# Sliding-window attention with a channel mix: crossbar transposes for two more batches, other loads for batch 0, mix copies shared between two engines, new orders

## The chip, the cores and the metric

One core of one Trainium2 chip. The metric is the device time of one launch in microseconds (us), lower is better. The engines are TensorE (PE, its weight load is PEld), VectorE (DVE), ScalarE (ACT), GpSimd (POOL) and SyncE (SP); SP issues hardware DMAs, POOL issues software DMAs, which can change the type on the way.

## The reference

Eight batches, eight heads, 576 positions, head size 64. Attention first, then a channel mix on its output (all inputs are fp32):

```python
scores = scale * q @ k.T ; bias = -slope[h] * |i - j| ; mask = 0 <= i - j < 128
attn = softmax(where(mask, scores + bias, -1e9)) ;  a = attn @ v
x = a.transpose(0, 2, 1, 3).reshape(B, S, 512)
x_prev = x shifted by one position, zero first
xk = mu_k * x + (1 - mu_k) * x_prev ;  xr = mu_r * x + (1 - mu_r) * x_prev
out = sigmoid(xr @ w_r) * (relu(xk @ w_k) ** 2 @ w_v)
```

## The kernel before, in words

**Pairs.** Attention works on pairs of heads: pair `it` is batch `it // 4`, group `it % 4`, 32 pairs in all. For each pair: scores in two halves (`scores` L229 with the distance bias as a matmul on L217 for batch 0; `scores4` L242, L247 for batches 2 and later), `expo` (L263) on ScalarE, `masked` (L271) on VectorE from batch 1 on, `av` (L287), then `norm`: a reciprocal of the row sums (L297) and a multiplication (L298) into the tile xu.

**From xu to the mix.** The normalised pair must be turned, so that features lie on partitions. In batches 0 to 3 (`NXB = 4`) TensorE does it with five 128x128 transposes (`x_transp`, L306) into PSUM, and ScalarE copies the result to xt (`x_copy`, L317). From batch 4 on one DMA through the crossbar does both (`x_cross`, L311, issued by SP). Then, on VectorE, `delta` (L330) is x less x shifted by one, `scaled` (L336) makes the two copies mu_k * delta and mu_r * delta, and `mix` (L347) adds the shifted x and writes xm, the input of the channel mix. In batch 0 the pair goes through this in two halves, of 256 and 320 positions.

**Units.** Two batches (1152 positions) make one P, 0 to 3. `mm1` (L359) multiplies by w_k in pieces of columns (four of 256, 256, 256, 384 in P = 0, then 512, 384, 256), eight output blocks each; `relu` (L365) on ScalarE; `square` (L372 on ScalarE or L374 on VectorE); `mm3` (L381) and `gate` (L387); `mm2` (L396); `product` (L402) on VectorE; `store` (L408) on SP.

**q and k.** From batch 2 on POOL loads them with a cast, VectorE turns them (`turn` L180, `turn_tail` L188) and SP shifts the turned queries with a DMA within SBUF (`shift`, L196, qt<-qt in the profile). In batches 0 and 1 TensorE transposes them (`qk_transp`) and ScalarE or VectorE copies them out of PSUM (L132, L129). Pair 0 alone (`NHW = 1`) comes as fp32 by SP (L93) and is cast on VectorE (L129); pairs 1 to 3 come cast, by POOL (L108, L124).

**Buffers.** Four PSUM banks "mm" serve transposes, mm1, mm2 and mm3 in turn; two pairs of banks "sa" serve scores and av. Delta and scaled copies have a ring of three tiles each, relu's tile rl four, the output tile ot three, xu three.

**Order.** The order on each engine is written out by hand in the tables ORDER (one list of names for each of PE, ACT, DVE, POOL, SP); a planner merges the lists with the dependences and gives out ring slots. `tq.5` is the transpose of pair 5's queries, `rl.0.256.3` the relu of P 0, columns from 256, block 3; `fill` is two matmuls on a tile of zeros. Whether a square runs on ScalarE is told by the list that holds its name. An engine works through its list strictly: an instruction that waits holds all behind it.

Of the kernel before, what the change touches and what calls it, by code (L numbers as in the profile page):

```python
# [16 lines left out]
def kernel(  # L17
# [12 lines left out]
    nc = tc.nc  # L30
# [16 lines left out]
    NXB = 4  # L47
# [6 lines left out]
    NHW = 1  # L54
# [5 lines left out]
    rlp = ctx.enter_context(tc.tile_pool(name="rlp", bufs=4))  # L60
    otp = ctx.enter_context(tc.tile_pool(name="otp", bufs=3))
# [21 lines left out]
    ldr = xk_buf[1][:, 0:2048].bitcast(FP32).rearrange("p (i g h c) -> p i g h c", i=2, g=NHW, h=2)  # L83
    ts_buf = xk_buf[1][:, 2048:2560].rearrange("p (h d) -> p h d", h=H)
    tt_buf = xk_buf[1][:, 2560:3328].rearrange("p (g t c) -> p g t c", g=G, t=3)
    cs_buf = [xr_buf[1][:, 1024 * i:1024 * i + 1024].rearrange(
        "p (i r h d) -> p i r h d", i=2, r=NF, h=2) for i in range(NHW)]
    dl_buf = [cst.tile([128, S], BF16, name=f"dl{i}") for i in range(3)]
    mb_buf = [cst.tile([128, 2, S], BF16, name=f"mb{i}") for i in range(NMB)]


    def load_qk(g, i):
        nc.sync.dma_start(  # L93
            out=ldr[:, i, g],
            in_=(q, k)[i][0, 2 * g:2 * g + 2, 0:SM].rearrange("h (p r) d -> p h (r d)", p=128))
# [195 lines left out]

    def norm(it, t0, t1):
        n = t1 - t0
        a5 = T.pop(("av", it, t0))[:, :, 0:n * W].rearrange("p h (t c) -> p h t c", c=W)
        rc = xup.tile([128, 2, NJ], FP32, tag="rc", name="rc")
        xu = T["xu", it, t0] = xup.tile([128, NJ, 2, D], BF16, tag="xu", name="xu")
        nc.vector.reciprocal(out=rc[:, :, 0:n], in_=a5[:, :, :, D])  # L297
        nc.vector.tensor_tensor(  # L298
            out=xu[:, t0:t1].rearrange("p t h d -> p h t d"), in0=a5[:, :, :, 0:D],
            in1=rc[:, :, 0:n, None].to_broadcast([128, 2, n, D]), op=ALU.mult)  # L300
# [717 lines left out]
```

## Time and profile before

| | |
|---|---|
| time, median of 3 runs | 230.58 us (230.04 to 230.89) |
| the profiled execution | 231.78 us, its span 229.9 us |
| busy in the span | PE 218.2, DVE 190.4, ACT 172.7, POOL 76.4 us |
| granted TensorE clock | 1.00 |
| HBM read, written | 33.56 MB, 9.44 MB |

The span is what the profile shows between first and last instruction. A row of groups gives line, engine, operation, out<-in, shapes, count, then busy time of the group in us and the mean of one in ns, then the idle time of the engine ahead of them and what ended it. A row of the chain or of the timeline starts with the start and the length in us.

### The profile page before, as it was taken

How to read it: one execution, taken by the hardware profiler on the slowest of the kernel's cores; microseconds unless marked ns; L12 is line 12 of the kernel's file. 1: busy time of each engine (PE TensorE's matmuls, PEld its weight loads, DVE VectorE, ACT ScalarE, POOL GpSimd, SP SyncE). 2: the span in 40 equal slices, each digit the busy share in tenths (PEclk: the TensorE clock that was granted, in tenths of full speed). 3: DMA queues.
4: the chain of work that ended last, by engine and by line, in shares of the span. 5: the costliest groups of instructions: out<-in, count | busy, mean ns of one | idle time of the engine just before them, and what ended most of it. 6: DMA issues, size and time to landing. Idle time of an engine off the chain costs nothing.

```text
span 229.9 us, 5654 instructions
## 1 busy us (share of the span) xinstructions
PE 218.2 (95%) x2226; PEld 128.1 (56%) x2261; DVE 190.4 (83%) x397; ACT 172.7 (75%) x326; POOL 76.4 (33%) x118
## 2 busy tenths in 40 slices
PE   7789989998999999999999999999999999999993
PEld 3446648755766555655566655556565465456541
DVE  7239999999899999999999999999989984761132
ACT  3968999996898997895699896868588668038810
POOL 8989864436565753271139100000000000000000
PEclk9999999999999999999999999999999999999999
DMA  5999999999999999999969996153422124240023
GB/s 112 164 145 157 175 157 201 209 172 182 228 199 185 182 210 199 155 134 208 114 128 112 220 141 146 33 165 128 91 80 74 48 56 120 99 152 26 0 98 130
DMA packets 83225, 31.82 MB, mean 138 GB/s; under 512 B 55032, under 2 KB 78592, under 8 KB 83200
## 3 DMA queue, kind: packets, MB, share of 16 engines
q0 software_dynamic: 61904, 16.52, 79.9%
q1 hardware_dynamic: 21296, 14.95, 25.8%
q8 instruction: 17, 0.28, 0.5%
q14 instruction: 8, 0.07, 0.1%
HBM read 33.56 MB, written 9.44 MB: 187 GB/s over the span
## 4 chain that ended last, share of the span: by engine, by line
PE 74%; DMA 10%; DVE 8%; POOL 3%; issue 1%; ACT 1%; SPq 1%; DVEq 0%; POOLq 0%
PE ps L359 25%; PE pv L396 22%; PE pr L381 11%; PE sa L287 6%; PE sa L242 4%; DMA qt<-qt 4%; DMA out_dram<-ot 3%; DMA vs<-in_v_dram 3%; DVE mb L336 2%; PE xp L306 1%; DVE xm L347 1%; PE sa L229 1%; DVE dl L330 1%; DVE xu L298 1%; PE sa L217 1%
## 5 line engine op out<-in xcount | busy, mean ns | idle before, releaser
L263 ACT ACTIVATE at<-sa 128x1024 bf16<-128x1024 f32 x64 | 64.0, 1031 | 13.7 <-PE sa L247 10.0
L359 PE MATMUL ps<-xm,wk_sb 128*128 128x256 bf16 (+2 forms) x412 | 70.4, 313 | 0.9 <-DVE xm L347 0.6
L396 PE MATMUL pv<-wv_sb,kk 128*128 128x512 bf16 x274 | 66.6, 379 | 0.8 <-issue 0.3
L365 ACT ACTIVATE rl<-ps 128x256 bf16<-128x256 f32 (+2 forms) x104 | 46.1, 474 | 14.0 <-PE ps L359 13.2
L359 PEld LDWEIGHTS <-wk_sb 128*128 128x128 bf16 x416 | 38.9, 98 | 22.5 <-issue 0.2
L396 PEld LDWEIGHTS <-kk 128*128 128x128 bf16 x288 | 26.9, 98 | 28.7
L372 ACT ACTIVATE kk<-rl 128x256 bf16<-128x256 bf16 (+2 forms) x79 | 38.4, 512 | 0.3
L271 DVE TENSOR_TENSOR at<-at,mask 128x1024 bf16<-128x1024 bf16 x56 | 36.9, 680 | 0.9 <-ACT at L263 0.8
L402 DVE SCALAR_TENSOR_TENSOR ot<-rs,pv 128x512 f32<-128x512 bf16 x36 | 24.4, 681 | 14.4 <-PE pv L396 10.5
L381 PE MATMUL pr<-wr_sb,xm 128*128 128x512 bf16 x131 | 35.2, 379 | 0.7
L99 POOL DMA_DIRECT2D vs<-in_v_dram x32 | 28.6, 902 | 20.1 <-PE sa L287 11.1
L387 ACT ACTIVATE rs<-pr 128x512 bf16<-128x512 f32 x36 | 21.3, 605 | 17.3 <-PE pr L381 17.1
L287 PEld LDWEIGHTS <-at 128*128 128x128 bf16 x576 | 21.6, 98 | 6.5 <-issue 1.0
L347 DVE TENSOR_TENSOR xm<-mb,xt 128x1152 bf16<-128x1152 bf16 (+3 forms) x40 | 24.4, 631 | 0.1
L298 DVE TENSOR_TENSOR xu<-sa,rc 128x640 bf16<-128x640 f32 x28 | 23.1, 824 | 1.0
L336 DVE TENSOR_SCALAR mb<-dl,mu_sb 128x576 bf16<-128x576 bf16 (+2 forms) x72 | 23.5, 386 | 0.2
L381 PEld LDWEIGHTS <-xm 128*128 128x128 bf16 x144 | 13.3, 98 | 12.3
L287 PE MATMUL sa<-vs,at 128*128 128x65 bf16 x448 | 18.8, 194 | 0.0
L242 PE MATMUL sa<-qt,kt 32*128 32x256 bf16 (+1 forms) x384 | 15.7, 266 | 1.2 <-DMA qt<-qt 0.7
L124 POOL DMA_DIRECT2D ql<-in_k_dram x15 | 11.7, 778 | 14.7 <-DVE kt L180 9.7
L374 DVE TENSOR_TENSOR kk<-rl 128x256 bf16<-128x256 bf16 (+2 forms) x25 | 8.0, 330 | 8.1 <-ACT rl L365 8.1
L330 DVE TENSOR_TENSOR dl<-xt 128x576 bf16<-128x576 bf16 (+2 forms) x36 | 14.6, 415 | 0.0
(72 smaller groups left out, 208.9 us busy)
## 6 DMA issues: line engine op xcount, KB each, us to landing
out_dram<-ot SPq DMA_DIRECT2D x36, 256.0 KB, 2.5
vs<-in_v_dram POOLq DMA_DIRECT2D x32, 128.0 KB, 8.3
ql<-in_k_dram POOLq DMA_DIRECT2D x15, 256.0 KB, 7.3
ql<-in_q_dram POOLq DMA_DIRECT2D x15, 256.0 KB, 7.6
qt<-qt SPq DMA_DIRECT2D x12, 192.0 KB, 6.8
wk_sb<-in_moe_w_k_dram POOLq DMA_DIRECT2D x2, 512.0 KB, 7.9
wv_sb<-in_moe_w_v_dram POOLq DMA_DIRECT2D x2, 512.0 KB, 13.2
tv<-in_v_dram POOLq DMA_DIRECT2D x8, 64.0 KB, 7.8
```

The lines of the kernel that those rows point to most:

```text
L99: nc.gpsimd.dma_start(out=vs_buf[b % NLD][:, j, :, 0:D], in_=v[b, :, 128 * j:128 * j + 128, :].rearrange("h p d -> p h d"))
L263: nc.scalar.activation(out=to, in_=sa, func=AF.Exp, scale=float(scale))
L271: nc.vector.tensor_tensor(out=a, in0=a, in1=m, op=ALU.mult)
L287: nc.tensor.matmul(pa[:, hl, W * (t - t0):W * (t - t0) + W], lhsT=at[:, lo:lo + 128], rhs=vs[:, u, 2 * g + hl, :] if u < NF else tvb[:, 2 ...
L298: nc.vector.tensor_tensor(out=xu[:, t0:t1].rearrange("p t h d -> p h t d"), in0=a5[:, :, :, 0:D], in1=rc[:, :, 0:n, None].to_broadcast([12 ...
L336: nc.vector.tensor_scalar(out=mb[:, w, c0:c1], in0=T["dl", it][:, c0:c1], scalar1=mu_sb[:, NPO * w + g:NPO * w + g + 1], scalar2=None, op0 ...
L347: nc.vector.tensor_tensor(out=xm_buf[P % 2][:, w0:w1, o:o + c1 - c0], in0=T["mb", it][:, w0:w1, c0:c1], in1=x_of(it, c0 - 1, c1 - 1)[:, No ...
L359: nc.tensor.matmul(ps[:, 0:c1 - c0], lhsT=wk_sb[:, po, 128 * fo:128 * fo + 128], rhs=xk[:, po, c0:c1], start=(po == 0), stop=(po == NPO - 1))
L365: nc.scalar.activation(out=rl[:, 0:c1 - c0], in_=T.pop(("ps", P, c0, fo))[:, 0:c1 - c0], func=AF.Relu, scale=RELU_SCALE)
L372: nc.scalar.activation(out=out_, in_=in_, func=AF.Square)
L381: nc.tensor.matmul(pr, lhsT=T["xr", P][:, po, 128 * c:128 * c + 128], rhs=wr_sb[:, po], start=(po == 0), stop=(po == NPO - 1))
L396: nc.tensor.matmul(pv, lhsT=kk[:, fo, o:o + 128], rhs=wv_sb[:, fo], start=(fo == 0), stop=(fo == NFO - 1))
```

## The change

- `NXB` 4 to 2: batches 2 and 3 (pairs 8 to 15) also take the crossbar DMA. TensorE's L306 and ScalarE's L317 of these eight pairs go; SP has 24 such DMAs in place of 16.
- `NHW` 1 to 4: q and k of all four pairs of batch 0 are eight fp32 loads on SP. Eight casts follow, six on VectorE, two on ScalarE (`c.1.1`, `c.3.1`). The tiles of pairs 2 and 3 lie in the buffer that later takes batch 2's q and k, so the load of these waits for the casts. The four POOL loads of the before go, and TensorE transposes a pair with four 128-wide transposes in place of eight 64-wide ones.
- `norm` is two operations in the tables, `rc` (the reciprocal, which takes the xu slot) and `norm`, and other work can stand between them.
- `scaled` is two operations, `ma` (mu_k) and `mr` (mu_r), each on VectorE or, as `activation(Copy, scale=mu)`, on ScalarE. 30 of the 56 of pairs 4 to 31 and seven of batch 0's stand in ScalarE's list.
- Rings: delta lies in the same tile as the two copies (ring of three); rl has three tiles, ot four; three tiles for casts.
- All five tables are new. VectorE's list has 42 squares, before 25; ScalarE's 62, before 79.

```diff
-    NXB = 4
+    NXB = 2
-    NHW = 1
+    NHW = 4
+    NCS = 3
-    rlp = ctx.enter_context(tc.tile_pool(name="rlp", bufs=4))
-    otp = ctx.enter_context(tc.tile_pool(name="otp", bufs=3))
+    rlp = ctx.enter_context(tc.tile_pool(name="rlp", bufs=3))
+    otp = ctx.enter_context(tc.tile_pool(name="otp", bufs=4))
...
-    dl_buf = [cst.tile([128, S], BF16, name=f"dl{i}") for i in range(3)]
-    mb_buf = [cst.tile([128, 2, S], BF16, name=f"mb{i}") for i in range(NMB)]
+    mb_buf = [cst.tile([128, 3, S], BF16, name=f"mb{i}") for i in range(NMB)]
...
+    def recip(it, t0, t1):
+        n = t1 - t0
+        a5 = T["av", it, t0] = T["av", it, t0][:, :, 0:n * W].rearrange(
+            "p h (t c) -> p h t c", c=W)
+        rc = T["rc", it, t0] = xup.tile([128, 2, NJ], FP32, tag="rc", name="rc")
+        T["xu", it, t0] = xup.tile([128, NJ, 2, D], BF16, tag="xu", name="xu")
+        nc.vector.reciprocal(out=rc[:, :, 0:n], in_=a5[:, :, :, D])
...
-    def scaled(it, c0=0, c1=S):
-        mb, g = ring_of("mb", mb_buf, it, c0), it % G
-        for w in range(2):
-            nc.vector.tensor_scalar(out=mb[:, w, c0:c1], in0=T["dl", it][:, c0:c1],
-                                    scalar1=mu_sb[:, NPO * w + g:NPO * w + g + 1], scalar2=None,
-                                    op0=ALU.mult)
+    def scaled(it, w, act, c0=0, c1=S):
+        mb, i = T["mb", it], NPO * w + it % G
+        mu = mu_sb[:, i:i + 1]
+        if act:
+            nc.scalar.activation(out=mb[:, w, c0:c1], in_=mb[:, 2, c0:c1], func=AF.Copy, scale=mu)
+        else:
+            nc.vector.tensor_scalar(out=mb[:, w, c0:c1], in0=mb[:, 2, c0:c1], scalar1=mu,
+                                    scalar2=None, op0=ALU.mult)
...
-            lq.0.0 lmu.0 lq.0.1 lmu.1 sh.2.0 sh.2.1 st.0.1 st.0.0 sh.3.0 st.0.2 sh.3.1
+            lq.0.0 lq.0.1 lq.2.0 lq.1.0 lq.1.1 lq.2.1 lq.3.0 lq.3.1 lmu.1 lmu.0 sh.2.0
+            sh.2.1 xt.8 sh.3.0 st.0.0 st.0.3 xt.9 sh.3.1 xt.10 xt.11 sh.4.0 st.0.1
```

**Three places in the orders.** First, ScalarE from the start of the program, before. The mask rows are make_mask, qt<-tp copies turned q or k out of PSUM, at<-sa is an exponential.

```order
L456 ACTIVATE mask<-dist 128x384 x4
L132 COPY qt_90<-tp 128x512
L456 ACTIVATE mask<-dist 128x384 x4
L263 ACTIVATE at_81<-sa 128x2x512
L132 COPY qt_90<-tp 128x512 x5
```

The same stretch now; the CAST is one of the two casts that ScalarE has.

```order
L460 ACTIVATE mask<-dist 128x384 x6
L128 COPY qt_90<-tp 128x512
L460 ACTIVATE mask<-dist 128x384 x2
L128 COPY qt_90<-tp 128x512 x2
L128 CAST xm_97<-xm_97 128x2x4x64
L259 ACTIVATE at_81<-sa 128x2x512
```

The first exponential stands behind all mask pieces, three copies and a cast, where before one copy and the masks were ahead of it.

Second, VectorE ahead of the first matmuls of the channel mix (tile ps), before. mb<-dl is a scaled copy, xm<-mb,xt the mix, at<-at,mask the mask of a pair of batch 1; the first ps needs the four mixes of 320 positions.

```order
L271 TENSOR_TENSOR at_82<-at_82,mask 128x2x512
L347 TENSOR_TENSOR xm_96<-mb_103,xt_94 128x320
L330 TENSOR_TENSOR dl_99<-xt_94 128x320
L347 TENSOR_TENSOR xm_96<-mb_103,xt_94 128x256
L336 TENSOR_SCALAR mb_102<-dl_99,mu_sb 128x320 x2
L347 TENSOR_TENSOR xm_96<-mb_102,xt_94 128x256
L330 TENSOR_TENSOR dl_98<-xt_94 128x320
L347 TENSOR_TENSOR xm_96<-mb_102,xt_94 128x320
```

The same place now, the twelve instructions up to the mix (the last row) that the first ps waits for; xu<-sa,rc is a division of batch 1.

```order
L298 TENSOR_TENSOR xu<-pa,rc 128x2x2x64
L351 TENSOR_TENSOR xm_96<-mb_98,xt_94 128x576
L341 TENSOR_SCALAR mb_99<-mb_99,mu_sb 128x576
L267 TENSOR_TENSOR at_84<-at_84,mask 128x2x512
L351 TENSOR_TENSOR xm_96<-mb_98,xt_94 128x256
L351 TENSOR_TENSOR xm_96<-mb_100,xt_94 128x256
L351 TENSOR_TENSOR xm_96<-mb_98,xt_94 128x320
L294 RECIPROCAL rc<-sa 128x10
L332 TENSOR_TENSOR mb_98<-xt_94 128x256
L298 TENSOR_TENSOR xu<-sa,rc 128x2x5x64
L332 TENSOR_TENSOR mb_100<-xt_94 128x320
L351 TENSOR_TENSOR xm_96<-mb_98,xt_94 128x256
```

The first ps now waits for the mixes of 256 positions. Five masks (one of them among these rows), a division of batch 1 and, further ahead, two turns of batch 2 stand before the last of these; in the old order one mask did, and the others came behind.

Third, VectorE from the first division of batch 2 (pair 9, first row) to its delta (last row), before; ot<-rs,pv is a product.

```order
L298 TENSOR_TENSOR xu<-sa,rc 128x2x5x64
L297 RECIPROCAL rc<-sa 128x10
L298 TENSOR_TENSOR xu<-sa,rc 128x2x5x64
L188 STREAM_TRANSPOSE qt_90<-kl_88 32x8x2x32
L402 SCALAR_TENSOR_TENSOR ot<-rs,pv 128x512
L180 STREAM_TRANSPOSE qt_90<-ql_80 128x4x4x32
L330 TENSOR_TENSOR dl_100<-xt_94 128x576
```

Now, from the division of pair 9 (first row) to the delta of pair 8 (last row). The division of pair 8 stands two rows ahead of these, with a turn between.

```order
L298 TENSOR_TENSOR xu<-sa,rc 128x2x5x64
L176 STREAM_TRANSPOSE kt_86<-ql_80 128x4x4x32
L176 STREAM_TRANSPOSE qt_90<-ql_80 128x4x4x32
L406 SCALAR_TENSOR_TENSOR ot<-rs,pv 128x512
L267 TENSOR_TENSOR at_84<-at_84,mask 128x2x512
L406 SCALAR_TENSOR_TENSOR ot<-rs,pv 128x512
L267 TENSOR_TENSOR at_84<-at_84,mask 128x2x512
L294 RECIPROCAL rc<-sa 128x10
L184 STREAM_TRANSPOSE kl_88<-kl_88 32x8x2x32
L298 TENSOR_TENSOR xu<-sa,rc 128x2x5x64
L294 RECIPROCAL rc<-sa 128x10
L332 TENSOR_TENSOR mb_100<-xt_94 128x576
```

Twelve instructions now stand between a pair's division and its delta; in the old order it was five.

More of the change, by code (lines that the diff above doesn't have):

```diff
@@ L135, in next_cs @@
         T["ncs"] = T.get("ncs", -1) + 1
-        return cs_buf[T["ncs"]]
+        return cs_buf[T["ncs"] % NCS]
     def cast_qk(g, i, f):
@@ L759, in add_pair, with scale_op @@
         vdep = [("lvs", b, j) for j in range(NJ)]
+        def scale_op(name, w, deps, c0=0, c1=S):
+            act = name in ON_ACT
+            op(name, "ACT" if act else "DVE", 280, lambda: scaled(it, w, act, c0, c1), deps, n,
+               uses=[("dl", it, 0) if b == 0 else ("dl", it)])
         got = []
```

361 lines of the change are left out of this document (182 added, 179 removed).

## The prediction

> **What bounds the kernel now.** First the busy shares, then the slices of the span (tenths of each of 40 slices), then the chain of waits.
>
> ```profile
> PE 218.2 (95%) x2226; PEld 128.1 (56%) x2261; DVE 190.4 (83%) x397; ACT 172.7 (75%) x326; POOL 76.4 (33%) x118
> PE   7789989998999999999999999999999999999993
> DVE  7239999999899999999999999999989984761132
> ACT  3968999996898997895699896868588668038810
> DMA  5999999999999999999969996153422124240023
> PE 74%; DMA 10%; DVE 8%; POOL 3%; issue 1%; ACT 1%; SPq 1%; DVEq 0%; POOLq 0%
> ```
>
> TensorE is busy from about 40 us to the end, and its matmuls hold 74% of the chain that ended last. VectorE is full beside it to about 160 us, and the DMA engines are full to about 115 us. The table by stages says how full, and the list of waits what still stops TensorE (time, times, longest).
>
> ```profile
> 10.00:20.00 10.00, 8.13 (x117) 4.43 (x116) 4.49 (x15) 7.52 (x12) 8.69 (x17) 1.00 2.31 156
> 40.00:60.00 20.00, 19.14 (x212) 13.21 (x214) 19.06 (x38) 17.23 (x38) 10.87 (x14) 1.00 1.70 200
> 60.00:80.00 20.00, 19.79 (x227) 12.00 (x228) 19.62 (x36) 18.16 (x37) 12.13 (x16) 1.00 1.79 188
> 80.00:100.00 20.00, 19.75 (x216) 11.21 (x219) 19.74 (x33) 17.98 (x32) 9.00 (x12) 1.00 1.37 176
> 200.00:220.00 20.00, 19.89 (x116) 11.44 (x117) 7.42 (x17) 11.87 (x29) 0.00 (x0) 1.00 0.14 53
> PEld L242 <- DVE xu L298: 1.2, 3, 0.5
> PEld L242 <- DVE at L271: 1.0, 1, 1.0
> PE ps L359 <- DVE xm L347: 0.6, 1, 0.6
> ACT rl L365 <- DVE kk L374: 0.6, 2, 0.4
> ```
>
> In 60 to 100 us PE (first number behind the length) is busy 39.5 of 40 us, VectorE (third) 39.4, ScalarE (fourth) 36.1. So the middle and the end move only with TensorE's own work and with the little that it waits; the rest can come from the start, where TensorE spends its time on matmuls of zeros and on waiting. Two rows bracket that start: the first mm1, and the first score of batch 2.
>
> ```profile
> L359 PE MATMUL ps<-xm,wk_sb x412: 269/326/390, 31.4 to 215.2; 128*128 128x256 bf16 x68, 128*128 128x384 bf16 x41, 128*128 128x512 bf16 x29
> L242 PE MATMUL sa<-qt,kt x384: 240/270/285, 46.2 to 178.5; 32*128 32x256 bf16 x144, 32*128 32x192 bf16 x48
> ```
>
> mm1 begins at 31.4 us, score.8 at 46.2. I compare the two kernels at score.8: when it starts, and how much of mm1 and mm3 is done by then.
>
> **Term 1, the transposes.** The chain gives the pitch of work that TensorE does back to back.
>
> ```profile
> 72.24 0.56 PE xp L306 x10
> 37.50 0.44 PE ps L359 x4
> 38.80 0.55 PE sa L287 x18
> 74.77 0.86 PE pr L381 x4
> ```
>
> Ten transposes take 0.56 us. The change drops 8 pairs of 5, so 40 x 0.056 = 2.2 us of a full engine: -2.2 us. They lie in 57 to 101 us, where PE has no room, so the time is gained in full as long as nothing new stops it. Batch 0's 24 narrow pairs of transposes become 24 wide ones; TensorE is not full there: 0.
>
> **Term 2, the start.** Three things could set the first mm1, which now waits for the mixes of 256 positions. What v needs:
>
> ```profile
> 8.58 6.69 DMA vs<-in_v_dram
> L99 POOL DMA_DIRECT2D vs<-in_v_dram x32 | 28.6, 902 | 20.1 <-PE sa L287 11.1
> L124 POOL DMA_DIRECT2D ql<-in_k_dram x15 | 11.7, 778 | 14.7 <-DVE kt L180 9.7
> ```
>
> POOL's list now has, from 1.6 us to the end of issuing batch 0's v: four v at 0.90, two q or k at 0.78, and six small loads and the memsets, about 6.2 us together: 1.6 + 3.6 + 1.6 + 6.2 = 13.0 us. The last v so starts at 12.1 and lands 6.7 us later as in the chain's row, at 18.8, or up to 21 us, since SP's eight fp32 loads of 256 KB now use the same DMA engines. I take 20.5. Then av and the first long reciprocal follow, at 20.9. From there VectorE's list has 37 instructions to the last mix that mm1 needs. Their lengths:
>
> ```profile
> L271 DVE TENSOR_TENSOR at<-at,mask 128x1024 bf16<-128x1024 bf16 x56 | 36.9, 680 | 0.9 <-ACT at L263 0.8
> L180 DVE STREAM_TRANSPOSE kt<-ql 128x512 f32<-128x512 f32 x12 | 13.2, 1103 | 0.0
> L298 DVE TENSOR_TENSOR xu<-pa,rc 128x384 bf16<-128x384 f32 x4 | 2.2, 557 | 0.1
> L336 DVE TENSOR_SCALAR mb<-dl,mu_sb 128x576 bf16<-128x576 bf16 x56 | 18.8, 385 | 0.2
> L347 DVE TENSOR_TENSOR xm<-mb,xt 128x256 bf16<-128x256 bf16 x4 | 1.1, 281 | 0.0
> 37.61 0.82 DVE L298 TENSOR_TENSOR xu<-sa,rc 128x640 bf16<-128x640 f32 x1
> 38.35 0.21 DVE L297 RECIPROCAL rc<-sa 128x10 f32<-128x10 f32 x1
> ```
>
> Five masks 3.4, two turns 2.2, four divisions of 384 2.2, the pair's division 0.82 and one of 256 0.42, six reciprocals 1.2, four scaled copies 1.4, and 15 deltas, mixes and a small copy of 0.27 on average (a mix of 256 has 0.28), 4.1: 15.7 us. The next instruction starts 0.74 us after the division of 0.82, so each overlaps the next by some 0.06: 37 x 0.06 = 2.2 off, 13.5. The last mix ends at 34.4; with 0.4 for one wait on an exponential and 0.2 to TensorE, mm1 begins at **35.0 us**. ScalarE would allow it earlier: its first relu stands here,
>
> ```profile
> 33.98 0.93 ACT L365 ACTIVATE rl<-ps 128x256 bf16<-128x256 f32 x3
> ```
>
> and two exponentials still followed. It now has six scaled copies more ahead of its first relu, about 2.4 us, as many copies and casts as before, and lost 2.5 us idle in 10 to 20 us (7.52 of 10), which the casts now fill. The scaled copy that mm1 needs stands 2.4 us ahead of that relu: about 33.4 us. So VectorE decides.
>
> From 35.0 to score.8 TensorE does eight blocks of mm1 (8 x 0.44), two av (1.1), four pairs' transposes (1.1) and three mm3 (2.6): 8.3 us, with some 0.7 of waits for divisions and relus 9.0, so score.8 at 44.0. Before, score.8 came at 46.2, but with fourteen blocks of mm1 and four mm3 done, 6 x 0.44 + 0.86 = 3.5 us more. 44.0 + 3.5 - 46.2 = **+1.3 us**. Its ends: ScalarE's 33.4 gives -0.1, a v that lands 1.5 us later gives +2.8.
>
> **Term 3, the middle.** The rows for what moves between the two engines:
>
> ```profile
> L372 ACT ACTIVATE kk<-rl 128x512 bf16<-128x512 bf16 x20 | 12.3, 635 | 0.1
> L372 ACT ACTIVATE kk<-rl 128x384 bf16<-128x384 bf16 x23 | 12.0, 533 | 0.1
> L317 ACT COPY xt<-xp 128x576 bf16<-128x576 bf16 x12 | 7.6, 640 | 2.0 <-PE xp L306 2.0
> L374 DVE TENSOR_TENSOR kk<-rl 128x384 bf16<-128x384 bf16 x9 | 3.1, 354 | 7.6 <-ACT rl L365 7.6
> L129 DVE CAST xm<-xm 128x512 bf16<-128x512 f32 x2 | 0.9, 457 | 0.0
> ```
>
> VectorE loses 30 scaled copies of pairs 4 to 31 (18.8/56 = 0.34 each, 10.1 us) and 11 of batch 0's 16 copies (3.4 us in all, since two of the five left are whole), and gains 17 squares (0.35 each, 5.9 us), four casts (0.46) and two copies of q or k (0.69), 9.1 us. So it is 4.4 us shorter; in 40 to 100 us, where 15 copies go and four squares come, 3.8 of 58.4. On ScalarE a scaled copy of 576 lies between 0.64 (the copy of 576) and 0.69 (0.635 plus half the step from 384 to 512); I take 0.69. In 40 to 100 us ScalarE gains 15 x 0.69 = 10.4, loses 8 x 0.63 = 5.1 and three squares, 1.3: 53.4 becomes 57.4 of 60. Both engines then stand near 55 to 57 of 60, where VectorE had 58.4. The waits of TensorE that name VectorE, 2.8 us in the first three rows of waits, should shrink by a quarter: **-0.7 us**; bounds 0 and -2.0.
>
> The rule that speaks against this: the Trainium skill, "ScalarE: Activation LUTs", section "Rules for kernel authors", says to use VectorE and not ScalarE for a multiplication. Its cost for this size, with one pointer operand, would be an estimated 0.76 us, and ScalarE in this stage 58.5 of 60. The trace has no such copy; the row of squares says 0.69.
>
> **Term 4, the crossbar DMAs.** They replace a transpose and copy of about 1 us by a DMA in the loaded phase. Landing times (minimum, median, longest), first of xt (pairs 16 to 31, after 111 us), then of the shift, which SP issues all along, then of v.
>
> ```profile
> DMA to landing us min/median/max: 2.6/2.6/7.4
> DMA to landing us min/median/max: 2.7/6.8/8.1
> DMA to landing us min/median/max: 3.7/8.3/14.3
> ```
>
> I expect 6.8 to 8.1, as the shift's. Between division and delta of pair 8 VectorE has three turns, three more divisions or tail turns, two products, two masks and two reciprocals, about 7.7 us by starts. So pair 8 may hold VectorE up to 1 us, once; pair 9's delta stands 16 us behind its division, pairs 10 to 15 have 9 or more. The same count covers the third xu slot. For TensorE: 0; bounds 0 and +2. In the Trainium skill, "Advanced Engine Details and Errata", section "X-Bar Transpose (TRN2)", such a DMA is as fast as a regular one; no run shown has one in the loaded phase.
>
> **Rest.** Rings of rl and mb get tighter by one tile, ot looser; in the list of waits the ring of rl shows with 0.6 us in all (the row above): 0, bounds -0.5 and +0.5. The end has the same form: one mm2, a product and a store. 0.
>
> **Sum.** -2.2 + 1.3 - 0.7 = -1.6 us. On the profiled execution, 231.78 becomes 230.2 (span 228.3); that execution was 1.2 us above the median of the runs, and the median 230.58 becomes **229.0**.
>
> **The rivals.**
> 1. *The start pays more.* VectorE's list meets v at 19 us and mm1 begins at ScalarE's 33.4 (-0.1), and the middle loses the full 2.0: 230.58 - 2.2 - 0.1 - 2.0 = 226.3. For it: VectorE, 4.49 of 10 busy in 10 to 20 us, takes the casts there. Against it: POOL's list alone gives 18.8 us.
> 2. *v lands later, and the change is slower.* Eight fp32 loads, 2 MB, share the DMA engines with v, which the slices show full from 6 us on. From 22.1 us on the gain is gone (20.5 + 1.6). With a landing time of 11.4, midway between v's median of 8.3 and its longest of 14.3, the last v is there at 23.5: +3.0, 232.0. Against it: v stands earlier in POOL's list, behind two loads of q and k and not four.
> 3. *The crossbar lands late.* If it takes 12 us behind stores and shifts, pairs 8, 10 and 12 stop VectorE by 4 + 1 + 1 us, TensorE by half of that, and half of the middle's gain goes: -2.2 + 1.3 - 0.3 + 3.0 = +1.8, 232.4. It decides from 9 us on. Against it: 8.1 is the longest of the shift.
> 4. *ScalarE becomes the engine waited for.* At 57.4 of 60 its relus come late and the four mm banks stay full; half of the 4.0 us added reaches TensorE in place of the -0.7: 231.7. For it: the start of mm1 waits for relus already. This is how the rule of the Trainium skill named above would come out.
>
> **How the numbers follow.** Forecast 0.42, rival 1 0.20, rival 2 0.19, rival 3 0.08, rival 4 0.11. A measurement of this kernel can tell about 0.5%, 1.15 us: faster is below 229.4, slower above 231.7. The forecast's own range, 228.0 to 230.0, is three quarters on the faster side, and with rival 1 that makes 0.52. Same: the last quarter of the forecast, and half of rivals 2 and 4 where they fall short of their price, 0.25. Slower: the rest, 0.23. The range 226.0 to 232.4 takes in the ends of all terms but the sum of the worst.
>
> **What would show it.** Right: mm1 from about 35 us, score.8 near 44; L306 with 40 in place of 80; scaled copies on ScalarE near 0.69 us; xt landing 6 to 8 us for pairs 8 to 15 and VectorE's wait for it 1 us or less; PE at 99% from 46 us on. Wrong: score.8 after 45.6, or stretches of some us between 46 and 110 us where TensorE waits for xm or for a free bank.

## The result: slower by 3.7 %, and the profile after

| | before | after |
|---|---|---|
| median | 230.65 us | 239.41 us (238.58 to 243.86, 4 runs) |
| ratio to before, 95 % interval | | 1.037 [1.0335, 1.041] |
| profiled execution, span | 231.78, 229.9 us | 239.21, 237.4 us |

Ratios and their intervals leave out runs more than 1.5 % above the fastest run of the same kernel, while medians and ranges take in all runs, so that the two can say different things for a kernel that spreads widely.

From the page after, busy times, slices and the chain:

```profile
PE 220.8 (93%) x2166; PEld 128.0 (54%) x2197; DVE 184.0 (77%) x379; ACT 183.1 (77%) x338; POOL 75.1 (32%) x114
PE   7499989999999999589999999999999999999993
PEclk9769999999999999979999999999999999999999
PE 52%; DMA 20%; ACT 16%; issue 6%; DVE 2%; POOL 1%; POOLq 0%; ACTq 0%; SPq 0%
```

TensorE's work no longer holds 74 % of the chain but 52, DMA 20 and ScalarE 16. There are two dents in PE, at the start and in the 17th and 18th slice (95 to 107 us), and the granted clock falls behind each. The table by stages:

```profile
10.00:20.00 10.00, 9.13 (x91) 4.81 (x94) 3.92 (x8) 6.02 (x9) 7.30 (x14) 0.68 2.58 159
40.00:60.00 20.00, 19.48 (x231) 14.17 (x234) 19.11 (x43) 19.91 (x46) 11.05 (x15) 1.00 1.76 180
60.00:80.00 20.00, 19.56 (x217) 11.61 (x217) 19.11 (x31) 18.41 (x37) 11.36 (x15) 1.00 1.76 178
80.00:100.00 20.00, 17.64 (x182) 9.23 (x181) 15.68 (x29) 19.38 (x33) 5.85 (x8) 1.00 1.90 184
100.00:120.00 20.00, 17.96 (x194) 10.39 (x197) 18.59 (x31) 13.71 (x21) 4.88 (x8) 0.91 1.07 199
```

ScalarE is at 19.91 of 20 us in 40 to 60. In 80 to 120 us TensorE does 35.6 us, before 39.2. To see where the time went I count from the end, each weight load with the columns of its matmul, and compare the times at which both traces have the same work left (so the transposes that the changed kernel no longer does count in its favour from the start). It is 0.8 us behind at 47 us, 0.9 behind at 97, 6.3 behind at 107, and 7.5 at the end. The orders differ, so each of these is good to about 1 us. The largest loss, some 5 us, lies between 97 and 107 us. The list of waits for 90 to 110 us:

```profile
POOL ql L120 <- DVE qt L176: 7.6, 1, 7.6
...
DVE kt L176 <- DMA ql<-in_k_dram: 4.3, 1, 4.3
...
PE sa L238 <- DVE kt L176: 3.4, 1, 3.4
```

VectorE waits for a load of k (batch 4's second half; POOL issues it at 89.4 us, it lands at 100.5), and TensorE's scores wait for VectorE: a load is late. What the DMA queues did in 60 to 100 us, before (q0 is POOL's software queue, q1 SP's hardware queue; packets, MB, time that packets took as a share of 16 engines; packets in flight overlap, so shares pass 100 %):

```profile
DMA packets 23777, 7.28 MB, mean 182 GB/s; under 512 B 15741, under 2 KB 23128, under 8 KB 23771
q0 software_dynamic: 21447, 5.09, 138.6%
q1 hardware_dynamic: 2324, 2.10, 18.4%
vs<-in_v_dram POOLq DMA_DIRECT2D x10, 128.0 KB, 8.0
```

and after:

```profile
DMA packets 24433, 7.24 MB, mean 181 GB/s; under 512 B 18084, under 2 KB 23787, under 8 KB 24428
q0 software_dynamic: 17449, 3.93, 134.1%
q1 hardware_dynamic: 6979, 3.24, 48.3%
vs<-in_v_dram POOLq DMA_DIRECT2D x10, 128.0 KB, 11.5
xt<-xu SPq DMA_TRANSPOSE x8, 8.5
```

The total is the same, 182 and 181 GB/s. The hardware queue, with eight crossbar DMAs, has 18.4 % then 48.3 %, and the loads (q0) moved 3.93 MB where they had moved 5.09. That the loads moved less is no sign of the crossbar by itself, since POOL's list is another one: j_pe below has the same list, no crossbar in this stretch, and 3.93 MB too. What differs between those two is how long the loads take. The rows that belong to the prediction's other terms, from the timeline and the groups:

```profile
37.47 1.04 PE L363 MATMUL ps<-xm,wk_sb 128*128 128x256 bf16 x8
...
L339 ACT ACTIVATE mb<-mb,mu_sb 128x576 bf16<-128x576 bf16 x32 | 25.5, 815 | 2.5 <-DVE mb L332 2.5
...
L307 PE MATMUL xp<-ident,xu 128*128 128x128 bf16 x40 | 4.0, 219 | 0.1
```

mm1 begins at 37.47 us in this execution, a scaled copy of 576 on ScalarE takes 0.82 us, and half the transposes are gone, as planned.

### The profile page after: what moved, and what is told of

It reads as the page before. It is cut to its first block, busy times and chain, and to the rows that moved or that the text cites. A ratio compares the mean times of both kernels' runs of the same rounds, so it can differ in the third digit from the quotient of the medians.

```text
span 237.4 us, 5533 instructions
## 1 busy us (share of the span) xinstructions
PE 220.8 (93%) x2166; PEld 128.0 (54%) x2197; DVE 184.0 (77%) x379; ACT 183.1 (77%) x338; POOL 75.1 (32%) x114
## 4 chain that ended last, share of the span: by engine, by line
PE 52%; DMA 20%; ACT 16%; issue 6%; DVE 2%; POOL 1%; POOLq 0%; ACTq 0%; SPq 0%
PE pv L400 19%; PE ps L363 16%; PE pr L385 8%; ACT at L259 8%; DMA ql<-in_q_dram 5%; DMA ql<-in_k_dram 5%; DMA xt<-xu 4%; PE sa L283 4%; DMA xm<-in_k_dram 4%; DMA vs<-in_v_dram 3%; PE sa L238 3%; ACT mb L339 2%; ACT qt L128 2%; ACT rl L369 1%; ACT kk L376 1%
## 5 line engine op out<-in xcount | busy, mean ns | idle before, releaser
L259 ACT ACTIVATE at<-sa 128x1024 bf16<-128x1024 f32 x64 | 65.3, 1064 | 15.4 <-PE sa L243 11.3
L400 PE MATMUL pv<-wv_sb,kk 128*128 128x512 bf16 x280 | 67.6, 384 | 0.8 <-issue 0.3
L369 ACT ACTIVATE rl<-ps 128x256 bf16<-128x256 f32 (+2 forms) x104 | 47.2, 490 | 18.4 <-PE ps L363 17.2
L385 PE MATMUL pr<-wr_sb,xm 128*128 128x512 bf16 x131 | 34.8, 379 | 0.9 <-issue 0.3
L406 DVE SCALAR_TENSOR_TENSOR ot<-rs,pv 128x512 f32<-128x512 bf16 x36 | 24.1, 682 | 10.8 <-PE pv L400 10.0
L376 ACT ACTIVATE kk<-rl 128x256 bf16<-128x256 bf16 (+2 forms) x62 | 31.4, 529 | 0.1
L339 ACT ACTIVATE mb<-mb,mu_sb 128x576 bf16<-128x576 bf16 (+2 forms) x37 | 28.6, 796 | 2.5 <-DVE mb L332 2.5
L351 DVE TENSOR_TENSOR xm<-mb,xt 128x1152 bf16<-128x1152 bf16 (+3 forms) x40 | 24.9, 632 | 2.9 <-ACT mb L339 2.6
L391 ACT ACTIVATE rs<-pr 128x512 bf16<-128x512 f32 x36 | 22.1, 618 | 1.3 <-PE pr L385 1.1
L378 DVE TENSOR_TENSOR kk<-rl 128x256 bf16<-128x256 bf16 (+2 forms) x42 | 13.5, 332 | 11.2 <-ACT rl L369 10.9
L385 PEld LDWEIGHTS <-xm 128*128 128x128 bf16 x144 | 13.3, 98 | 13.4 <-issue 0.2
L332 DVE TENSOR_TENSOR mb<-xt 128x576 bf16<-128x576 bf16 (+2 forms) x36 | 14.8, 416 | 6.4 <-DMA xt<-xu 5.5
L176 DVE STREAM_TRANSPOSE kt<-ql 128x512 f32<-128x512 f32 x12 | 13.2, 1101 | 4.3 <-DMA ql<-in_k_dram 4.3
```

What stands on the lines that cost most here:

```text
L259: nc.scalar.activation(out=to, in_=sa, func=AF.Exp, scale=float(scale))
L339: nc.scalar.activation(out=mb[:, w, c0:c1], in_=mb[:, 2, c0:c1], func=AF.Copy, scale=mu)
L351: nc.vector.tensor_tensor(out=xm_buf[P % 2][:, w0:w1, o:o + c1 - c0], in0=T["mb", it][:, w0:w1, c0:c1], in1=x_of(it, c0 - 1, c1 - 1)[:, No ...
L369: nc.scalar.activation(out=rl[:, 0:c1 - c0], in_=T.pop(("ps", P, c0, fo))[:, 0:c1 - c0], func=AF.Relu, scale=RELU_SCALE)
L376: nc.scalar.activation(out=out_, in_=in_, func=AF.Square)
L385: nc.tensor.matmul(pr, lhsT=T["xr", P][:, po, 128 * c:128 * c + 128], rhs=wr_sb[:, po], start=(po == 0), stop=(po == NPO - 1))
```

## The experiments

Each edit is to the changed kernel, unless "the kernel before" is named. The names in the tables are those of ORDER.

### Is it the late load, by its place in POOL's list?

**a_load**

```diff
 POOL
-  lql.4.0.1 lvs.3.4 lvs.5.2 ... lvs.4.4 lql.4.1.1 lvs.4.0
+  lql.4.0.1 lql.4.1.1 lvs.3.4 lvs.5.2 ... lvs.4.4 lvs.4.0
```

> One entry moves: in POOL's list the load of batch 4's second k half stands before the four loads of v that follow batch 4's first halves, and no longer behind batch 6's tail. Theory 1 (this load's place is what costs most: TensorE's and VectorE's stop at 96 to 102 us and the half clock behind it, 5.1 us between equal points of the work in the two traces): 239.4 falls by 4.5 to 5.5 us, to about 234.4, TensorE has no wait above 1 us between 90 and 110 us and the granted clock of that stage is 1.00. Theory 2 (ScalarE, 19.9 of 20 us busy in 40 to 60 us, is the limit, and the stop only lets it catch up): the gain is under 2 us, 237.5 or more, and TensorE's waits for relus and exponentials take the place of the stop.

238.9 us (237.01 to 241.73), ratio 1.031 [1.024, 1.038]. The wait for k is gone and another stands in its place, in 40 to 130 us of this trace:

```profile
POOL vs L100 <- PE sa L283: 16.4, 2, 11.4
...
PE sa L283 <- DMA vs<-in_v_dram: 5.1, 2, 3.1
```

The third product of scores and v in batch 3 now waits for v. In POOL's list `lvs.5.2`, which needs batch 2's last av (69 us), stands ahead of two loads of batch 3's v. Theory 1 had one stop too few; theory 2's relus do not appear. So a third theory: the queue behind that one waiting load.

**f_v3** and **g_both**

```diff
 POOL, f_v3
-  lvs.3.4 lvs.5.2 lts.5.1 lvs.3.2 lvs.3.3 lvs.5.0
+  lvs.3.4 lvs.3.2 lvs.3.3 lvs.5.2 lts.5.1 lvs.5.0
 POOL, g_both
+  lvs.3.4 lvs.3.2 lvs.3.3 lql.4.1.1 lvs.5.2 lts.5.1 lvs.5.0
```

> In POOL's list of the changed kernel the two last loads of batch 3's v stand ahead of the load of batch 5's v that waits for batch 2's last av (until 68 to 69 us), and no longer behind it. Theory 3: the queue behind that one waiting load costs the time; which of its loads stops TensorE first, batch 3's v at 79 us or batch 4's k at 97 us, differs from run to run. With v ahead, its stop (5.1 us of TensorE's waits in the run with the k load moved) goes, and the k load, now two issues earlier, still stops TensorE by some 1.5 us: 239.4 falls by 1.5 to 3.5 us, to about 237. Rival (the DMA engines carry too much, whatever the order): batch 3's v still lands after 82 us, and the time stays within 1 us of 239.4.

> The two v loads of batch 3 and the k load of batch 4 all stand ahead of the load that waits for batch 2's last av. Theory 3: both stops go with their half clock, 5 to 7 us: about 233.5, with no wait of TensorE above 1 us and no granted clock under 1.00 between 60 and 120 us. Rival (ScalarE full, or the DMA engines): TensorE stops elsewhere, and the time stays above 236.

f_v3 240.3 us, 1.042 [1.035, 1.049]; g_both 239.2 us, 1.038 [1.0315, 1.044]. Neither gains. In f_v3 TensorE stops for the turn of batch 4's k again, for 6.9 us. In g_both TensorE now stops for batch 4's v (40 to 140 us):

```profile
POOL vs L100 <- DMA vs<-in_v_dram: 8.4, 5, 3.2
...
PE sa L283 <- DMA vs<-in_v_dram: 3.2, 1, 3.2
```

Whichever load is put first, the next one is late. POOL itself waits for earlier loads (8.4 us). Theory 3 falls as the main cause; its rival, the DMA engines, stands.

### The start and the half clock

**c_fill9**, **b_fill101**

```diff
-    FILL = (2,) * 14
+    FILL = (2,) * 13 + (9, 7)      # c_fill9:  ... fill.13 tq.1 fill.14 tail.0 ...
+    FILL = (2,) * 14 + (16,)       # b_fill101: ... m1.1.0.5 fill.14 score.18 ...
```

> Fourteen matmuls of zeros are added in the two waits of the start: seven before batch 0's second q transpose (idle 7.1 to 8.9 us) and seven before the transposes of the tail (9.1 to 10.8 us). If the half clock of 9.5 to 16.2 us comes from these waits and TensorE sets the start, the work of 10.8 to 16.2 us takes 2.7 us less and the time falls by 1.5 to 2.7 us, to about 237.3; the granted clock of 10 to 20 us is 1.00 in place of 0.68. If the start is set by loads and ScalarE (the rival: mm1's first matmul waits for the last v and for VectorE's list), the clock recovers and the time falls by 0.5 us or less.

238.5 us (237.16 to 245.46), 1.030 [1.027, 1.034]: by the ratio 0.7 %, 1.6 us, at the low end of what the first theory asked, and the interval touches that of the change. In its trace the clock of 10 to 20 us is 1.00 and mm1 begins at 34.9 us. But the fills may not be what did it: j_pe, k_half and t_pool below have the start of the change without them, and their traces too show a clock of 1.00 in 10 to 20 us and mm1 at 34.7 to 34.9.

> Sixteen matmuls of zeros (16 x 0.216 = 3.5 us) are added to TensorE's list ahead of score.18, where the changed kernel has TensorE idle for 3.6 us at 98 to 101.6 us. If the drop of the clock to a half behind that wait comes from the idle time and costs TensorE what its records show (half speed from 101.8 to 105.2 us, so 1.7 us of work), the time falls by 1.2 to 1.9 us, to about 237.8, with the granted clock of 100 to 120 us at 1.00 in place of 0.91. If VectorE and ScalarE, which were held by the same load, set the pace after it, or the drop has another cause, it stays within 0.5 us of 239.4.

243.6 us, 1.054 [1.049, 1.059]: 4.2 us slower, which nobody expected. In this trace the stop was not at 98 us but already at 79 to 82, for v, and the matmuls of zeros only added their 3.6 us:

```profile
82.03 0.38 PE L283 MATMUL sa<-vs,at 128*128 128x65 bf16 x4 [2.21 <-DMA vs<-in_v_dram]
102.64 3.62 PE L197 MATMUL wm<-zero 128*128 128x512 bf16 x16
```

So it says nothing of the clock, but something of the cause: up to that place the program is the changed one, and its stop is at another load than in the first trace.

**d_tail**, **i_start** (the latter with g_both's list)

```diff
 PE
-  fill.13 tq.1 tail.0 score.0.0 score.0.1
+  fill.13 tq.1 score.0.0 tail.0 score.0.1
```

> In TensorE's list the first scores of batch 0 stand before the transposes of its tail and no longer behind them; the tail's load landed at 10.7 us. If the first exponential (12.84 us) was late because of that place, it comes at about 10.5 us, the waits of the start shrink, and the time falls by 1.5 to 2.5 us, to about 237.4, with less of the half clock in 10 to 20 us (0.68). If the last v and VectorE's list set the first mm1, the exponentials come earlier, mm1 stays within 0.7 us of 37.5 us and the time falls by 0.5 us or less.

> As the last kernel, and the first scores ahead of the tail's transposes in TensorE's list. Theory 3 says that the earlier start was hidden by the stop for batch 3's v, which came at the same time whatever the start; with that stop gone, the start's gain (first exponential 10.3 in place of 11.7 to 12.8 us, equal work 0.5 to 2.0 us earlier) shows in the time: 0.5 to 2 us under the last kernel, about 232.3. Rival (ScalarE, full from 20 to 60 us, sets the pace to 60 us): within 0.4 us of the last kernel.

d_tail: 239.9 us (236.18 to 244.57), 1.028 [1.021, 1.034]; the first exponential is at 10.26 us, mm1 at 35.5, the clock of 10 to 20 us 1.00, and TensorE then waits 5.1 us for v. i_start: 237.0 us (233.2 to 241.65), 1.015 [1.009, 1.021]; three runs lie at 233 to 235, three at 239 to 242. If the start has a price, it is 1 to 2 us, and these spreads do not settle it. That the same program lies 8 us apart from run to run is itself new: the kernel before had 230.0 to 232.6 us in 13 runs of one series, and 234.7 at most in any.

### The crossbar by itself

**e_xbar**

```diff
 the kernel before
-    NXB = 4
+    NXB = 2
 PE   - ot.8 ... ot.15      ACT  - xt.8 ... xt.15
 SP   + sh.3.0 xt.9 xt.8, sh.3.1 xt.10 xt.11, st.0.5 xt.12 xt.13, st.0.6 xt.15 xt.14
 DVE  + mask.11.0 dl.9 ma.9, norm.11 dl.8
```

> The kernel before, with the crossbar DMAs for pairs 8 to 15 alone: 40 transposes and eight copies on ScalarE go, eight DMAs are added in SP's list, and the differences of pairs 8 and 9 stand some instructions later in VectorE's list; nothing else changes. If the transposes are worth what the prediction said (40 x 0.056 us), the time falls by 1.5 to 2.5 us from 231.2, to about 229.0. If the DMA comes late in the loaded phase, or its traffic delays the loads of batches 4 and 5, VectorE waits for x by 2 us or more in all and the time is 231 to 233.

244.8 us (244.62 to 246.89), 1.062 [1.056, 1.0675]: 14 us slower. This one part is worse than the whole change. Its waits in 40 to 140 us:

```profile
DVE dl L330 <- DMA xt<-xu: 14.0, 3, 7.1
...
PE sa L242 <- DMA qt<-qt: 4.1, 2, 3.4
```

VectorE waits 14 us for x in three places, and the shift on the same queue comes late too. In the changed kernel's orders the differences stand further behind the divisions, and in its trace VectorE waits for x once ahead of 100 us, 0.6 us.

**m_xb8**, **n_plain8**, **v_xb8late**

```diff
 the kernel before
+    def x_dummy(i):
+        nc.sync.dma_start_transpose(out=spare..., in_=wr_sb[...])     # m_xb8, v_xb8late
+        nc.sync.dma_start(out=spare..., in_=wr_sb[...])               # n_plain8
 SP   + two each behind sh.3.0, sh.3.1, st.0.5, st.0.6                 # m_xb8, n_plain8
 SP   + two each behind xt.24, st.1.8, st.2.0, st.2.2                  # v_xb8late
```

> The kernel before with eight crossbar DMAs added in SP's list at the places of pairs 8 to 15 (two each behind four of its entries, about 57 to 95 us), from wr_sb to a tile that nobody reads; all transposes stay on TensorE. It does more than the reference asks. Theory 4: 12 us of full DMA time, less what the loads have in hand: 4 to 10 us slower than 231, 235 to 241. Rival (the lateness of x and the waits for it were the cost, not the traffic): nobody waits for these, so 231 to 232.

> The same eight DMAs with the same bytes at the same places, as plain copies of rows of 1280 bytes and not as transposes. Theory 4 says that the 256-byte packets are the cost, not the bytes: as the trace has 96 ns for a packet of 2048 and 40 for one of 512, 128 rows are about 128 x 0.07 = 9 us of one engine, 0.55 us of all, 4.5 us for eight: 0 to 2.5 us slower than 231. If bytes or the eight further issues on SP are the cost, it is as slow as the kernel with eight crossbar DMAs.

> The kernel before with the same eight added crossbar DMAs that nobody reads, which cost 7 us at 57 to 100 us, issued behind 150 us, where the DMA engines are busy for less than 0.6 of a slice. It does more than the reference asks. Theory 4 (a crossbar costs what it delays in full DMA engines): 231 to 231.8, no slower than 0.4%. Rival (each holds SP's queue, or stops all the cores' DMA, wherever it stands): it delays the crossbars of pairs 25 to 31 and stores, 2 us or more slower.

m_xb8: 237.8 us (236.15 to 242.83), 1.030 [1.020, 1.040]. n_plain8: 231.35 us, 1.0006 [0.997, 1.004]. v_xb8late: 232.1 us, 1.007 [1.004, 1.010]. Nobody reads what these DMAs write. The same bytes as plain copies cost nothing, as transposes in the loaded phase 7 us (4.6 to 9.2 by the interval), and late 1.6 us (0.2 each), more than expected but a quarter. They land in 8.5 us (median) in the loaded phase and in 2.7 us late. The queues in 60 to 100 us, with transposes:

```profile
DMA packets 25680, 7.40 MB, mean 185 GB/s; under 512 B 18626, under 2 KB 25164, under 8 KB 25676
q0 software_dynamic: 19832, 4.70, 126.6%
q1 hardware_dynamic: 5844, 2.64, 39.7%
```

and with plain copies:

```profile
DMA packets 24640, 8.49 MB, mean 212 GB/s; under 512 B 15676, under 2 KB 23995, under 8 KB 24635
q0 software_dynamic: 21174, 5.03, 132.1%
q1 hardware_dynamic: 3461, 3.39, 30.5%
```

The plain copies come on top, 212 GB/s and 5.03 MB of loads; with transposes the total stays at 185 and the loads lose 0.39 MB. From the packet records of 55 to 105 us: 4814 packets of 256 bytes on the hardware queue took 208.8 us (43 ns each, 27.8 us for the 640 of one transpose), 1024 packets of 1280 bytes took 71.5 us (70 ns each, 8.9 us for one copy). The Trainium skill, "Advanced Engine Details and Errata", section "X-Bar Transpose (TRN2)", calls transposing DMAs as fast as regular ones; here one takes three times the engine time of a copy of the same size. In m_xb8's trace TensorE has no wait for the shift, though that is on the crossbars' queue. The stop is of the same kind as in the changed kernel: VectorE's turn of k, for which TensorE's scores wait, waits for its load, which it never does in 40 to 140 us of the kernel before:

```profile
DVE kt L180 <- DMA ql<-in_k_dram: 4.3, 2, 3.2
```

**u_noxt**

```diff
 the kernel before
+        if b in (2, 3):
+            pass                       # no transpose, no copy
-           ... delta ... [("xt", it)]
+           ... delta ... [("norm", it) if b in (2, 3) else ("xt", it)]
```

> The kernel before without the transposes and copies of pairs 8 to 15, and without anything in their place: the differences of these pairs read what batches 0 and 1 left in the x tiles, so the output of batches 2 and 3 is left out. This is what the crossbar could bring at best. The prediction's first term says 40 x 0.056 us of a full TensorE: 2.2 us faster, 228.0 to 229.0. If TensorE's time there is held by VectorE or ScalarE (both near 20 of 20 us), 0.5 us or less.

231.5 us (230.34 to 233.41), 1.001 [0.9975, 1.005]: nothing, the second answer. The 80 to 120 us rows of its table by stages show where it went:

```profile
80.00:100.00 20.00, 20.00 (x219) 10.72 (x215) 19.72 (x35) 17.22 (x29) 11.29 (x15) 1.00 1.45 182
100.00:120.00 20.00, 17.89 (x191) 10.50 (x189) 18.20 (x34) 13.28 (x26) 4.00 (x6) 1.00 0.94 146
```

With the same work left, TensorE keeps some 2 us of the 2.2 to 102 us in this run, and loses 1.8 again by 115: it does 17.9 us in the next stage (before 19.46), in waits for a product that waits for a store, and for a division on VectorE. So the best that the crossbar could bring here was about nothing, -0.6 to +1.1 us.

### Taking the crossbar out of the change, and ScalarE

**j_pe** and **k_half**

```diff
-    NXB = 2
+    NXB = 4      # j_pe: ot.8-15 back on PE, xt.8-15 on ACT
+    NXB = 3      # k_half: ot.8-11 back on PE, xt.8-11 on ACT
```

> The changed kernel with the transposes of pairs 8 to 15 back on TensorE and their copies on ScalarE; all else as changed. Theory 4: the crossbar DMAs are the cost. In the trace of the changed kernel the four of 60 to 80 us are 2560 packets of 256 bytes that take 94.4 us of one DMA engine's time, 23.6 each, so 1.5 us of all 16; eight are 12 us, put into a phase in which the slices of the page before show the DMA engines full to about 95 us, and every load behind them lands later. Then the time falls from 239.4 by 5 to 8 us, to 231.5 to 234.5, although TensorE does 2.2 us more and ScalarE eight copies more. Rival (the order of POOL's list and a full ScalarE): with more work on ScalarE and the same POOL list the stops stay, 238 or more.

> As the last kernel, with pairs 8 to 11 on TensorE and pairs 12 to 15 still by crossbar DMA. Theory 4: half the DMA time, and the earlier half gone: 2 to 4 us above the last kernel, 234 to 237. If it is the first crossbars (pairs 8 to 11, ahead of batch 3's v) that cost, within 1 us of the last kernel; if the crossbar costs nothing, equal to it or 1 us faster.

j_pe: 238.5 us (235.58 to 240.73), 1.024 [1.015, 1.033]. k_half: 234.2 us (233.15 to 234.62), 1.013 [1.008, 1.019]. With half the crossbars the kernel is 5.2 us faster than the change, and its four runs lie within 1.5 us: that speaks for the first four, ahead of batch 3's v, as the costly ones. But without any it is no better, above the range expected for j_pe.

The stop itself does go with the crossbars. First VectorE's turn of batch 4's k in the changed kernel, then the same turn in j_pe, and j_pe's queue and loads in 60 to 100 us, to compare with the rows after the change above:

```profile
100.52 1.08 DVE L176 STREAM_TRANSPOSE kt<-ql 128x512 f32<-128x512 f32 x1 [4.32 <-DMA ql<-in_k_dram]
...
96.50 1.07 DVE L176 STREAM_TRANSPOSE kt<-ql 128x512 f32<-128x512 f32 x1
...
q0 software_dynamic: 17748, 3.93, 108.2%
vs<-in_v_dram POOLq DMA_DIRECT2D x10, 128.0 KB, 7.9
```

With the same list on POOL and the same 3.93 MB, the loads' packets take 108.2 % and not 134.1, v lands in 7.9 us and not 11.5, POOL issues that load of k at 83.6 us and not 89.4, and the turn does not wait. The other traces of the changed kernel and its variants agree. In 60 to 110 us seven of the eight with eight crossbars (the change, a_load, b_fill101, c_fill9, d_tail, f_v3, g_both; not i_start) have TensorE stopped for 3 to 7 us in all by loads of q, k or v, directly or through VectorE's turn of k. Of the six with four or none (j_pe, k_half, and q_k_dve, r_j_dve, s_best and t_pool below) none waits for such a load, nor for a turn that does. So the late loads of the changed kernel are the crossbars' doing. What j_pe loses in its place I can show only in part: in its trace TensorE has no wait over 1.6 us in 58 to 110 us, yet falls 2 to 3 us behind there, and another 1 us behind 160 us.

**q_k_dve** and **r_j_dve** (on k_half and j_pe)

```diff
 ACT  - ma.p, mr.p of pairs 4 to 31 (30 names)
 DVE  + each just ahead of xk.p
```

> As the kernel with crossbar DMAs for pairs 12 to 15 alone (234.2), and the 30 scaled copies of pairs 4 to 31 that ScalarE has go back to VectorE, each just ahead of its pair's mix. Rival 4 of the prediction (ScalarE, at its limit in 20 to 60 us, holds TensorE's banks): ScalarE falls by 30 x 0.8 us, VectorE gains 30 x 0.34, and the time falls by 1.5 to 3 us, to about 232. If the rest of the loss is the start and the DMA engines, the time stays within 0.7 us of 234.2, or rises by 1 to 2 us since VectorE is full again (its list then is 5.8 us longer than before's in copies of the start).

> The same on the kernel that has all transposes of pairs 8 to 15 on TensorE (238.5; its profiled run 235.6): no crossbar ahead of 105 us and no scaled copy of pairs 4 to 31 on ScalarE, so that of the change the start, the orders and the tiles are left. If ScalarE was what kept it slow (it had the eight copies out of PSUM as well): 232 to 234, and steadier from run to run. If the start and POOL's order are: 235 to 238.

q_k_dve: 239.1 us (238.19 to 239.39), 1.035 [1.031, 1.039]; r_j_dve: 238.1 us (237.96 to 239.91), 1.033 [1.028, 1.038]. On k_half, the copies back on VectorE cost 4.9 us; on j_pe they are no gain. To 110 us q_k_dve's trace is level with k_half's, both 0.8 to 0.9 us behind the kernel before, so ScalarE's load was not the cost there. The loss comes between 110 and 140 us, behind an entry of POOL's list that waits 13.4 us; TensorE then waits for a load that stood behind it (tv, the tail of v), in r_j_dve too (1.5 us):

```profile
POOL vs L100 <- PE ps L363: 14.5, 2, 13.4
...
PE sa L283 <- DMA tv<-in_v_dram: 3.0, 1, 3.0
```

So these two runs hold a cost of POOL's list, and do not price the copies by themselves.

### All that helped

**s_best** (k_half, d_tail, g_both together) and **t_pool** (k_half, g_both's list, and one more entry)

```diff
 POOL, t_pool
-  lql.6.1.1 lvs.7.3 lql.7.0.1 lql.7.0.0 lvs.6.3 lvs.5.4 lvs.6.4 lvs.6.0
+  lql.6.1.1 lql.7.0.1 lql.7.0.0 lvs.6.3 lvs.5.4 lvs.6.4 lvs.6.0 lvs.7.3
```

> Crossbar DMAs for pairs 12 to 15 alone, the first scores ahead of the tail's transposes, and the loads of batch 3's v and batch 4's k ahead of the load that waits: all edits so far that could help, together. Theory 4 with the start and the queue as smaller terms: 1 to 2.5 us under 234.2, about 232.3, still no faster than before. Rival (start and queue cost nothing once the DMA engines are free): 234.2 within 0.7 us.

> As the kernel with crossbar DMAs for pairs 12 to 15 alone (234.2), and POOL's list in another order: batch 3's last v and batch 4's k ahead of the load that waits for batch 2's last av, and the load of batch 7's v that waits for batch 4's last av (11.8 us, 101.8 to 113.6) behind six loads that need not wait. If what is left of the loss is loads queued behind a waiting one (theory 3, second place), the loads of batches 5 and 6 go out up to 12 us earlier, TensorE's and VectorE's waits of 118 to 145 us go, and the time falls by 1 to 2.5 us, to 231.7 to 233.2. If the order of the work or the start is what is left, it stays within 0.7 us of 234.2.

s_best: 237.55 us (233.93 to 242.33), 1.016 [1.010, 1.022], no gain over k_half. t_pool: 232.9 us (232.54 to 234.65), 1.008 [1.006, 1.011]: 1.3 us under k_half's median, though the intervals of the two overlap, and k_half's trace is of its slowest run, t_pool's of its fastest. In 120 to 140 us TensorE does 18.50 us in k_half (first row) and 20.00 in t_pool:

```profile
120.00:140.00 20.00, 18.50 (x211) 11.15 (x211) 17.58 (x33) 16.44 (x30) 5.75 (x7) 1.00 2.18 153
120.00:140.00 20.00, 20.00 (x229) 12.28 (x222) 19.16 (x36) 18.25 (x33) 2.44 (x3) 1.00 1.73 155
```

That speaks for a load that waits long for its buffer holding the others back, and for its place to count once the DMA engines have room. No version beat the kernel before.

## Why the prediction was wrong, step by step

- **Term 4, "For TensorE: 0; bounds 0 and +2", is the step that failed.** It priced the crossbar by when its own result lands (6.8 to 8.1 expected; eight in 60 to 100 us had a median of 8.5) and by who waits for x (1 us or less expected, 0.6 measured ahead of 100 us). Both came out nearly as said, and neither was the price. The price was on the loads that share the engines: 7 us with nobody waiting, and in the changed kernel a load of k that took 11.1 us to land and stopped TensorE. The slices quoted at the top of the prediction (DMA at 9 of 10 to about 115 us) were a bound that I used for landing times and never for the sum. Rival 3 named the culprit and gave it 0.08, but its path was wrong (VectorE waiting for x), so its price of 232.4 was too small.
- **Term 1, -2.2 us, was 0** (-0.6 to +1.1). That TensorE was at 99 % showed that it was busy, not that nothing else was as close: VectorE had 19.6 to 19.75 of 20 us in the same stage, and in u_noxt's trace the time gained was lost again in waits for a product and for a division on VectorE. "The time is gained in full as long as nothing new stops it" should have had its own bounds, from 0 to -2.2.
- **Term 2, the start, +1.3, did not fail.** 37.47 us for mm1 is this one execution. Seven other traces have the same program to 47 us (a_load, b_fill101, f_v3, g_both, j_pe, k_half, t_pool), and there mm1 begins at 34.7 to 36.0 and score.8 at 43.5 to 44.9, where 35.0 and 44.0 were expected. The work done by score.8 is that of the prediction, eight blocks of mm1 and three mm3, so the start costs 0.8 to 2.2 us there, and 3.6 in the profiled execution. In j_pe TensorE waits for v until 20.9 us, and the first long reciprocal and mm1 follow at 21.5 and 34.8. (The list that the prediction adds up has 38 instructions and not 37, and its two rows give an overlap of 0.08 us and not 0.06. From the reciprocal to mm1 it expected 14.1 us, and j_pe has 13.3.) This is mm1 in j_pe:

```profile
34.79 1.04 PE L363 MATMUL ps<-xm,wk_sb 128*128 128x256 bf16 x8
```

  In the profiled execution of the change, POOL's last issue of that v ended at 15.8 and not 13.0, since a load of batch 1's tail in the same list waited for TensorE's transposes of batch 0's tail, which waited for their own load until 10.8 us. There the half clock came on top, and the first long reciprocal stood at 24.2.
- **Term 3, the middle, -0.7:** the busy time came out (ScalarE 57.7 of 60 us in 40 to 100 us, 57.4 expected), though the scaled copy took 0.82 us, not 0.69; the prediction's estimate of 0.76 from the Trainium skill, "ScalarE: Activation LUTs", section "What ACT_TABLE_LOAD costs", was nearer. The gain did not: the kernel was as far behind at 97 us as at 47 (0.9 and 0.8). Rival 4, ScalarE as the engine waited for, is not borne out either: to 110 us, moving the copies back changed nothing in k_half.
- **Rest, 0:** the new order of POOL's list was not looked at beyond batch 0. Two of its entries wait 6 and 12 us with loads behind them. Moving them brought about 1.3 us in k_half, and with eight crossbars only chose which load is late.

**What adds up, and what does not.** Of the 8.8 us, taking four crossbars out brings 5.2 and POOL's list 1.3; 2 us are left in t_pool, in which half the crossbars and the start remain. Eight crossbars put into the kernel before cost 6.9. But these prices can't be added freely: without any crossbar ahead of 105 us, j_pe and r_j_dve are still 1.024 and 1.033 of the kernel before, 5.5 and 7.6 us, where the prediction's other terms say +0.6. So eight crossbars by themselves can cost most of what the change lost, and yet they are not all of it: the new start and orders lose time without them too. **Open:** where j_pe loses it, and why it is not faster than k_half; what part of a transpose's price is packet time and what a stop of other queues; and what the half clock behind a stop costs by itself.

## What to carry to other kernels

A DMA has two prices: when its result lands, and what it takes from the others while the engines are full; look at the slices of the DMA engines before moving work to a DMA, and test it by adding the DMA with no reader. An engine at 99 % is a bound only for work that no second engine at 98 % holds up: leave the work out, with nothing in its place, before writing a replacement. When repairing one wait moves the stop to the next load, suspect the rate of the loads before their order. And one profiled execution of a kernel that spreads by several us is one sample: compare the same stretch in other traces before explaining it.

## What the runs showed of the hardware

- A crossbar DMA of 128 x 640 bf16 within SBUF is 640 packets of 256 bytes, 43 ns each in the loaded phase, against 70 ns for a packet of 1280 bytes: 27.8 against 8.9 us of one engine's time. The 43 ns go with the load: 36 ns in the changed kernel in 55 to 105 us, 22 ns in v_xb8late behind 139 us, where few loads run beside them.
- TensorE's clock can fall to a half after a short wait too. In 2 us steps of the changed kernel's start (last numbers: clock, DMA share, GB/s):

```profile
6.00:8.00 2.00, 1.22 (x9) 0.44 (x7) 0.00 (x0) 2.00 (x6) 2.00 (x4) 1.00 1.35 274
8.00:10.00 2.00, 0.40 (x4) 0.23 (x4) 1.13 (x2) 1.39 (x4) 2.00 (x8) 0.87 1.28 263
10.00:12.00 2.00, 1.18 (x6) 0.56 (x6) 0.56 (x2) 0.41 (x1) 0.42 (x2) 0.50 1.33 246
16.00:18.00 2.00, 1.95 (x25) 0.89 (x22) 0.60 (x2) 1.47 (x3) 1.30 (x2) 0.92 4.08 95
```

A clock of 0.87 over 8 to 10 us is half speed for the last 0.5 us, so the clock fell at about 9.5 us. By then TensorE had waited 1.65 us (7.2 to 8.9 us), had done 0.4 us of transposes, and was 0.2 us into a second wait of 1.55 us. By the same reckoning (0.92 over 16 to 18 us) full clock came back at 16.3 us, after 5.5 us of unbroken work. The same start in k_half, with waits of 1.34 and 0.61 us, kept 1.00. The Trainium skill, "TensorE: Matmul & The Clock Gate", section "Part 1: The HAM clock gate", gives about 3.4 us of idle time as the window. Here less idle time went ahead of the drop than that.
